# x and u of a fused attention and mixer kernel: turned by the crossbar DMA and added as PSUM is read

## The chip, the core and the metric

The kernel runs on one core of one Trainium2 chip. The metric is device time in microseconds (us), the median of several executions; the profile is one further execution taken by the hardware profiler.

## The reference

Causal attention over 8 batches of 8 heads, 576 positions of 64 elements, with a decay from the running sum of `max(s, 0)`; its output x (8 x 576 x 512) goes through a low-rank mix over the sequence and a two-layer ReLU network, each with a residual:

```python
cum = np.cumsum(np.maximum(s, 0.0), axis=-1)
scores = scale * q @ k^T + np.minimum(-(cum[i] - cum[j]), 0.0)     # causal
attn = softmax(scores);  x = attn @ v                              # heads side by side: 512 wide
h = x.transpose(0, 2, 1) @ U @ V                                   # rank 32, over the 576 positions
u = x + h.transpose(0, 2, 1)
out = u + np.maximum(u @ w_ch1, 0.0) @ w_ch2                       # 512 -> 2048 -> 512
```

## The kernel before

**Attention, two heads at a time.** A pair n is two heads of one batch; there are 32 pairs, four per batch. For each head `diagonal` (token D, matmul at L254) and `below` (E, L254) make the transposed scores in PSUM. ScalarE exponentiates them into the tiles `pT` (d, f, m and, once a pair, l: L319). VectorE masks the diagonal blocks (k, K: L322). `values` (A, L333) multiplies with v in 15 small matmuls, and `divide` (a, L348 and L349) writes the normalised x in bf16 into `x_sb`, positions on the partitions.

**The mix, one pair (128 channels) at a time.** `mix_in` (U, L363) multiplies x by U in five matmuls; `mix_keep` (u, L374) copies the result `ux` out of PSUM. The transposed u of the pair is then built in PSUM as x^T plus the low-rank part. `mix_x` (X, L381) turns x with four matmuls against the identity, each 128 wide. `mix_out` (Y) turns the last 64 positions (L392) and adds `ux` times V on top (L401, 512 and 64 columns). `mix_done` (y, L408 and L409) copies the sum into `uT`, which holds u^T of all 8 batches.

**The network, 512 tokens at a time.** Nine groups g. `widen` (L418) makes 16 tiles of the hidden layer, four matmuls of 512 columns each, followed by a ReLU on ScalarE (L425) into `hT`. `narrow` makes four output tiles of 128 tokens: 16 matmuls of 512 columns each (L435), then four matmuls of u^T against the identity (L447), which put u itself, positions on the partitions again, on top of the sum. `finish` copies the sum out (L458) and SyncE stores it.

**What sets the order.** Instructions are recorded in an order written out by hand, and each engine runs its own in that order. `SEQ` is the order for batches 0 and 1, `PAIR` the step repeated for n = 8 to 33: in step n the scores and exponentials of pair n, the values of pair n-2 (A-2, A-1 for its two heads) and the mix of pair n-2. A token `F` lets the network go on by one piece (four matmuls of L418 or of L435); `e` does so from pair 16 on; `r` records the ReLU or the copy-out that such a piece left pending. `p` spins idle matmuls (L498) early on, to keep TensorE working. `G` records a VectorE transpose (L238) of later q and k and, after every second one, four SyncE DMAs (`slot<-turned`, L244). Four PSUM buffers `pscore` serve the scores, four buffers `pwork` all the rest.

**The queues.** GpSimd issues the loads of q, k, v and weights in the order of `LOADS`. SyncE issues, in program order, the slot DMAs (L244), the rows of the decay (L162) and the stores of the output (L459).

Of the kernel before, what the change touches and what calls it, by code (L numbers as in the profile page):

```python
# [16 lines left out]
ALU = mybir.AluOpType  # L17
# [3 lines left out]
def kernel(  # L21
# [63 lines left out]
    uT = consts.tile([128, 4, B * S], BF16)  # L85
    staged = [[], []]
    for c, src0 in enumerate((q_0, k_0)):
        staged[0].append([src0[:, 0:4, :], src0[:, 4:8, :]])
        staged[1].append(
            [  # L90
                uT[:TP, 2 * c + i, 2 * S : 2 * S + 4 * TT * D].rearrange("p (h t) -> p h t", h=4)
                for i in range(2)
            ]
        )
    spare = [uT[:, dt, 2 * S + 4 * TT * D : 2 * S + 4 * TT * D + 2 * S] for dt in range(3)]
# [246 lines left out]
    def divide(h):  # L342
        b = h // H
        if b not in x_of:
            x_of[b] = work.tile([128, 5, DM], BF16, tag="x_sb", name="x_sb")
# [3 lines left out]
        nc.vector.tensor_tensor(  # L349
            x_of[b][:, :, ds(h % H * D, D)],  # L350
            po[:, :, 0:D],
            rec.to_broadcast([128, 5, D]),
            op=ALU.mult,
        )

    def x_part(n, t):
        return x_of[n // PB][:, t, ts(n % PB, 128)]

    def mix_in(n):
        up = pwork()  # L360
# [16 lines left out]
    def mix_x(n):  # L377
        ut = pwork()
        mix_of[n].append(ut)
        for t in range(4):  # L380
# [6 lines left out]
                skip_group_check=True,  # L387
            )

    def mix_out(n):  # L390
        up, ux, ut = mix_of[n]
        nc.tensor.matmul(  # L392
            up[:, 128:192],
            lhsT=x_part(n, 4),
            rhs=identity[:, :64],
            start=True,
            stop=False,
            skip_group_check=True,
        )
        for dst, lo, hi in ((ut, 0, 512), (up[:, 128:192], 512, S)):  # L400
            nc.tensor.matmul(  # L401
                dst, lhsT=ux, rhs=V_sb[:, lo:hi], start=False, stop=True, skip_group_check=True
            )

    def mix_done(copy, n):
        up, ux, ut = mix_of.pop(n)
        b, hp = divmod(n, PB)
        copy(uT[:, hp, ds(b * S, 512)], ut)  # L408
        copy(uT[:, hp, ds(b * S + 512, 64)], up[:, 128:192])  # L409

    hidden = {}

    def widen(g):
        hT = hidden[g] = work.tile([128, NF, 512], BF16, tag="hT", name="hT")
        for nf in range(NF):
            f1 = pwork()
            for kt in range(4):
                nc.tensor.matmul(  # L418
                    f1,
                    lhsT=w1_sb[nf // 4][:, kt, ds(nf % 4 * 128, 128)],  # L420
                    rhs=uT[:, kt, ds(g * 512, 512)],
                    start=(kt == 0),
                    stop=(kt == 3),
                )
            pending.append(lambda nf=nf, f1=f1: nc.scalar.activation(hT[:, nf, :], f1, RELU))  # L425
            del f1
            yield

    def narrow(g):
        hT = hidden.pop(g)  # L430
        for i in range(4):
            f2 = pwork()
            tok = g * 512 + i * 128
            for nf in range(NF):
                nc.tensor.matmul(  # L435
                    f2,
                    lhsT=hT[:, nf, ds(i * 128, 128)],
                    rhs=w2_sb[nf // 4][:, nf % 4, :],
                    start=(nf == 0),
                    stop=False,  # L440
                    skip_group_check=True,
                )
                if nf % 4 == 3 and nf < NF - 1:
                    pending.append(None)
                    yield
            for dt in range(4):
                nc.tensor.matmul(  # L447
                    f2[:, ds(dt * 128, 128)],
                    lhsT=uT[:, dt, ds(tok, 128)],
                    rhs=identity,  # L450
                    start=False,
                    stop=(dt == 3),
                    skip_group_check=True,
                )

            def finish(f2=f2, tok=tok):
                o_sb = work.tile([128, DM], FP32, tag="o_sb", name="o_sb", bufs=3)
                nc.vector.tensor_copy(o_sb, f2)  # L458
# [56 lines left out]
    def queue(n):  # L515
# [18 lines left out]
        "a": divide,  # L534
        "U": mix_in,
        "X": mix_x,
        "Y": mix_out,
        "t": take,
        "u": mix_keep,
# [9 lines left out]
    def play(tokens, pair=None):  # L549
        for token in tokens.split():  # L550
# [8 lines left out]
            if pair is not None and kind in "DEdfmkAaTtlKUXYuyG":  # L559
# [101 lines left out]
    def begin_v(i):  # L661
# [18 lines left out]
    SEQ = (  # L680
# [12 lines left out]
    )  # L693
    PAIR = (
        "D0 d0 U-2 uV-2 X-2 F r E0 k0 f0 G1 m0 F r D1 d1 Y-2 yV-2 F r E1 k1 f1 G1 m1 l0 F r A-2 "
        "K0 a-2 e r A-1 a-1 F r F r e r "
    )

    with tc.manual_schedule():
# [14 lines left out]
        queue(100 + NG - 1)  # L714
        while feed():
            follow()
        follow()


# [28 lines left out]
```

## Time and profile before

| what | value |
|---|---|
| median of 3 runs | 389.23 us (389.22 to 389.81) |
| the profiled execution's own time | 392.76 us |
| its span, first to last instruction | 391.0 us |
| mean granted TensorE clock | 0.978 |
| DMA packets | 76158, 36.79 MB |

A profile's page gives busy time by engine, the span in 40 slices, the DMA queues, the chain of work that ended last, and groups of instructions by line. Each row of a group reads: line, engine, operation, tiles, shapes and count, then busy time and the mean duration of one, then the idle time ahead of it and who ended that. The duration of a matmul is its whole passage through the array; matmuls overlap, so what one costs TensorE is the distance from start to start in the timeline. A windows view gives busy time of each engine in a stretch, the granted clock, and the DMA's share.

### The profile page before, as it was taken

To read this page: it belongs to the slowest core of one execution; us is meant where nothing else is said; L and a number is where in the kernel's file an instruction comes from. 1 tells how busy PE (TensorE), PEld (TensorE's weight loads), DVE (VectorE), ACT (ScalarE), POOL (GpSimd) and SP (SyncE) were. 2 spreads that over 40 slices of the span, in tenths; PEclk is the share of its full clock that TensorE was granted. 3 is DMA by queue.
4 is the path that set the end of the run, shared out by engine and by line. 5 is a ranking of instruction groups with operands and counts; after the bars stand their busy time and mean duration, and the time that the engine had idled before them with its cause. 6 is when DMAs were issued, how large, how long until landed. Compare 5 with 4: busy or idle time off the path is not lost.

```text
span 391.0 us, 8307 instructions
## 1 busy us (share of the span) xinstructions
PE 377.9 (97%) x3303; PEld 219.3 (56%) x3359; DVE 202.5 (52%) x429; ACT 207.7 (53%) x402; POOL 108.8 (28%) x175
## 2 busy tenths in 40 slices
PE   6998999999999999999999999999999999999995
PEld 2457557655666556555566555655655554444442
DVE  8348555795767676665566556655633332011011
ACT  7267899259634786347633773377337701611610
POOL 8795428147273072308040710000000000000000
PEclk9569999999999999999999999999999999999999
DMA  7999999469799589829682892211210002002002
GB/s 92 176 202 160 177 161 114 87 129 195 111 173 135 109 103 84 150 86 124 64 150 86 105 81 88 75 46 34 60 55 27 2 28 80 2 27 80 2 27 80
DMA packets 76158, 36.79 MB, mean 94 GB/s; under 512 B 60672, under 2 KB 67872, under 8 KB 76120
## 3 DMA queue, kind: packets, MB, share of 16 engines
q0 software_dynamic: 65616, 18.43, 52.5%
q1 hardware_dynamic: 10504, 17.83, 15.4%
q8 instruction: 26, 0.43, 0.5%
q14 instruction: 12, 0.10, 0.1%
HBM read 37.51 MB, written 10.03 MB: 122 GB/s over the span
## 4 chain that ended last, share of the span: by engine, by line
PE 90%; DVE 4%; DMA 2%; issue 2%; POOL 1%; SPq 0%; ACT 0%; ACTq 0%; POOLq 0%
PE pwork L418 31%; PE pwork L435 30%; PE pscore L254 11%; PE pwork L333 7%; PE pwork L363 2%; PE pwork L447 2%; PE pwork L401 2%; PE pwork L381 2%; DMA hT<-in_k_dram 1%; PE pscore L263 1%; DVE slot L224 1%; PE pwork L212 1%; DVE x_sb L349 1%; POOL hT L109 1%; DMA slot<-turned 1%
## 5 line engine op out<-in xcount | busy, mean ns | idle before, releaser
L319 ACT ACTIVATE pT<-pscore 128x512 bf16<-128x512 f32 (+1 forms) x224 | 113.3, 557 | 78.2 <-PE pscore L254 68.9
L418 PE MATMUL pwork<-uT,w_sb 128*128 128x512 bf16 x552 | 136.8, 379 | 2.0 <-DVE uT L408 0.7
L435 PE MATMUL pwork<-w_sb,hT 128*128 128x512 bf16 x547 | 135.2, 379 | 1.5
L425 ACT ACTIVATE hT<-pwork 128x512 bf16<-128x512 f32 x144 | 86.5, 605 | 70.2 <-PE pwork L418 68.7
L418 PEld LDWEIGHTS <-w_sb 128*128 128x128 bf16 x576 | 52.3, 98 | 50.3
L435 PEld LDWEIGHTS <-hT 128*128 128x128 bf16 x576 | 52.2, 98 | 50.3
L254 PE MATMUL pscore<-slot 128*128 128x128 bf16 (+5 forms) x576 | 70.1, 245 | 0.1
L458 DVE COPY o_sb<-pwork 128x512 f32<-128x512 f32 x36 | 24.9, 691 | 83.4 <-PE pwork L447 83.2
L254 PEld LDWEIGHTS <-slot 128*128 128x128 bf16 (+1 forms) x576 | 43.9, 99 | 32.3 <-issue 3.9
L238 DVE STREAM_TRANSPOSE turned<-qk_sd 128x576 bf16<-128x576 bf16 x48 | 54.6, 1141 | 0.7
L127 POOL DMA_DIRECT2D qk_sd<-in_q_dram x48 | 27.0, 570 | 96.8 <-DVE turned L238 90.6
L333 PEld LDWEIGHTS <-pT 128*128 128x128 bf16 x960 | 35.8, 98 | 9.3 <-issue 0.4
L333 PE MATMUL pwork<-v_slot,pT 128*128 128x65 bf16 x960 | 38.4, 193 | 0.3 <-DVE slot L224 0.3
L322 DVE TENSOR_TENSOR pT<-pT,keep 128x512 bf16<-128x512 bf16 (+1 forms) x84 | 29.3, 353 | 16.4 <-ACT pT L319 16.1
L349 DVE TENSOR_TENSOR x_sb<-pwork,rec 128x320 bf16<-128x320 f32 x64 | 31.5, 492 | 2.2
L408 DVE CAST uT<-pwork 128x512 bf16<-128x512 f32 x27 | 18.6, 690 | 24.7 <-PE pwork L401 24.7
L127 POOL DMA_DIRECT2D qk_sd<-in_k_dram x48 | 27.2, 573 | 8.9 <-DMA w_sb<-in_moe_w_ch_dram 5.1
L135 POOL DMA_DIRECT2D v_slot<-in_v_dram x32 | 28.4, 898 | 2.3 <-DMA v_slot<-in_v_dram 1.5
L224 DVE COPY slot<-pwork 64x576 bf16<-64x576 bf16 x21 | 16.5, 796 | 17.6 <-PE pwork L212 14.7
L374 DVE CAST ux<-pwork 128x128 bf16<-128x128 f32 x26 | 7.5, 287 | 26.5 <-PE pwork L363 26.5
L348 DVE RECIPROCAL rec<-pwork 128x5 f32<-128x5 f32 x64 | 12.2, 190 | 11.2 <-PE pwork L333 10.9
L447 PEld LDWEIGHTS <-uT 128*128 128x128 bf16 x144 | 11.1, 98 | 8.5
(80 smaller groups left out, 192.3 us busy)
## 6 DMA issues: line engine op xcount, KB each, us to landing
out_dram<-o_sb SPq DMA_DIRECT2D x36, 256.0 KB
slot<-turned SPq DMA_DIRECT2D x96, 72.0 KB
v_slot<-in_v_dram POOLq DMA_DIRECT2D x32, 128.0 KB, 6.9
w_sb<-in_moe_w_ch_dram POOLq DMA_DIRECT2D x8, 512.0 KB, 11.7
qk_sd<-in_q_dram POOLq DMA_DIRECT2D x48, 72.0 KB, 3.8
qk_sd<-in_k_dram POOLq DMA_DIRECT2D x48, 72.0 KB, 4.0
uT<-in_q_dram POOLq DMA_DIRECT2D x2, 288.0 KB, 8.1
uT<-in_k_dram POOLq DMA_DIRECT2D x2, 288.0 KB, 9.0
```

The source lines that it names most:

```text
L127: nc.gpsimd.dma_start(out=qk_t[g][ds(32 * a, 32), c, :].rearrange("p (n f) -> p n f", n=6), in_=src[g // 2, 4 * (g % 2) + a].rearrange("(n ...
L135: nc.gpsimd.dma_start(out=vt[:, t, :, 0:D], in_=v[b, :, ds(t * 128, 128), :].rearrange("h p d -> p h d"),)
L238: nc.vector.transpose(turned[:, e, c].rearrange("p (n m t) -> p n t m", n=6, t=3), src[:, c].rearrange("p (n t e d) -> p e n t d", n=6, t= ...
L254: nc.tensor.matmul(dst, lhsT=head_of(h)[0:rows, ds(S + j * 128, 128)], rhs=head_of(h)[0:rows, lo:hi], start=start, stop=stop and not bias, ...
L319: nc.scalar.activation(dst, src, EXP, scale=scale)
L322: nc.vector.tensor_tensor(p, p, m, op=ALU.min)
L333: nc.tensor.matmul(po[:, i, :], lhsT=p_of(h)[:, ds(spot(j, i), 128)], rhs=v_slots[h // H % 3][:, j, h % H, :], start=(j == 0), stop=(j == ...
L349: nc.vector.tensor_tensor(x_of[b][:, :, ds(h % H * D, D)], po[:, :, 0:D], rec.to_broadcast([128, 5, D]), op=ALU.mult,)
L418: nc.tensor.matmul(f1, lhsT=w1_sb[nf // 4][:, kt, ds(nf % 4 * 128, 128)], rhs=uT[:, kt, ds(g * 512, 512)], start=(kt == 0), stop=(kt == 3),)
L425: pending.append(lambda nf=nf, f1=f1: nc.scalar.activation(hT[:, nf, :], f1, RELU))
L435: nc.tensor.matmul(f2, lhsT=hT[:, nf, ds(i * 128, 128)], rhs=w2_sb[nf // 4][:, nf % 4, :], start=(nf == 0), stop=False, skip_group_check=True,
L458: nc.vector.tensor_copy(o_sb, f2)
```

## The change

**x.** From batch 2 on (n >= 8) the five matmuls that turn x (L381, L392) are gone. A new token `x` (`turn_x`) has SyncE issue one crossbar transpose per pair, a DMA from `x_sb` (128 x 640, bf16) to one of three buffers `xT`. `mix_out` now starts its PSUM sum from `ux` times V alone, and `mix_done` adds `xT` on VectorE as it reads PSUM. `x_sb` is laid out by pair, so that a pair's x is contiguous.

**u.** From group 1 on (UB = 1) the four matmuls per output tile that put u on the sum (L447) are gone. At the start of `widen(g)` SyncE issues one crossbar transpose per group, from `uT` (128 x 2048) to one of two buffers `u_sb`; `finish` adds `u_sb` on VectorE as it reads PSUM.

**Buffers.** `uT` now holds a ring of four groups instead of all batches; the 576 columns of a pair are cut where a group ends, so the two matmuls with V have 384 and 192 columns in batch 2, 320 and 256 in batch 3, and so on, instead of 512 and 64. The second batch's staging of q and k lies in the new tile `stage`, whose space the transposes use later; scratch rows of the decay have tiles of their own.

**Orders.** `SEQ` and `LOADS` are other orders of nearly the same tokens: idle spins are 25 matmuls instead of 17 (first eight and five and four; now twelve ahead of the first q and k transposes, eight behind them, then three and two), and weights w3, w2 and w1 come ahead of the second half of batch 1's q and k. In `PAIR` both D0 and E0 come first, the network goes on in threes rather than by one, `x-1` follows the division of the pair one step younger than the one that is mixed, and Y and y stand late in the step; `ux` is copied by ScalarE (uA) instead of VectorE (uV).

```diff
+    uT = consts.tile([128, 4, 4, 512], BF16)
+    stage = consts.tile([128, 16 * TT * D], BF16, name="stage")
+    u_sb = [stage[:, ts(i, 2048)].rearrange("p (d i c) -> p d i c", d=4, i=4) for i in range(2)]
...
+    def turn_x(n):
+        nc.sync.dma_start_transpose(
+            out=xT[n % 3], in_=x_of[n // PB][:, n % PB].rearrange("p t c -> p (t c)")
+        )
...
+        mixed = n >= 2 * PB
+        cut = 512 - 64 * (n // PB)
+        if mixed:
+            mix_of[n].append(pwork())
...
+        for dst, lo, hi in pieces:
+            nc.tensor.matmul(
+                dst, lhsT=ux, rhs=V_sb[:, lo:hi], start=mixed, stop=True, skip_group_check=True
+            )
...
+                if b >= 2:
+                    turned = xT[n % 3].rearrange("p t c -> p (t c)")
+                    nc.vector.tensor_add(dst, got[:, p - lo : e - lo], turned[:, p:e])
+                else:
+                    copy(dst, got[:, p - lo : e - lo])
...
+    def turn_u(g):
+        nc.sync.dma_start_transpose(
+            out=u_sb[g % 2].rearrange("p d i c -> p (d i) c"),
+            in_=uT[:, g % 4].rearrange("p d c -> p (d c)"),
+        )
...
     def widen(g):
+        if g >= UB:
+            turn_u(g)
...
-            for dt in range(4):
+            for dt in range(4 if g < UB else 0):
                 nc.tensor.matmul(
                     f2[:, ds(dt * 128, 128)],
...
+                    nc.vector.tensor_tensor(
+                        o_sb.rearrange("p (d c) -> p d c", d=4),
+                        f2.rearrange("p (d c) -> p d c", d=4),
+                        u_sb[g % 2][:, :, i, :],
+                        op=ALU.add,
+                    )
...
-        "v0 u0 s0 w0 u1 w1 k0 x0 s1 v2 w2 w3 v1 x3 x1 x2 q4 q5 "
+        "u1 v0 u0 k0 w0 s0 w3 w2 w1 s1 x2 v1 x0 x1 x3 q4 v2 q5 "
...
-        "p1 p3 p4 T0 p5 Z0 T1 tA0 tV1 T3 p4 T2 tA0 D0 tA2 tV1 E0 T5 d0 f0 tV3 tV2 m0 D1 tV3 d1 "
+        "p7 p5 Z0 T0 tA0 tA0 p8 T3 T1 tA1 T2 tV3 D0 d0 tV3 tV2 tA1 p3 E0 D1 p2 d1 T5 f0 E1 tV2 "
...
-        "D0 d0 U-2 uV-2 X-2 F r E0 k0 f0 G1 m0 F r D1 d1 Y-2 yV-2 F r E1 k1 f1 G1 m1 l0 F r A-2 "
-        "K0 a-2 e r A-1 a-1 F r F r e r "
+        "D0 E0 r d0 A-2 U-2 G1 r e k0 F a-2 G1 D1 r A-1 f0 uA-2 e r l0 d1 F m0 a-1 x-1 r F r E1 "
+        "f1 k1 Y-2 r e K0 r yA-2 m1 F F "
```

On VectorE, one step of the later batches, before (`ux` and the two copies into `uT` are L374, L408 and L409; the copy-out of an output tile is L458):

```order
L374 CAST ux<-pwork 128x128
L322 TENSOR_TENSOR pT_77<-pT_77,keep 128x512
L238 STREAM_TRANSPOSE turned<-qk_sd 128x6x3x32
L408 CAST uT<-pwork 128x512
L409 CAST uT<-pwork 128x64
L322 TENSOR_TENSOR pT_77<-pT_77,keep 128x512
L238 STREAM_TRANSPOSE turned<-qk_sd 128x6x3x32
L458 COPY o_sb<-pwork 128x512
L322 TENSOR_TENSOR pT_77<-pT_77,keep 128x2x64
L348 RECIPROCAL rec<-pwork 128x5
L349 TENSOR_TENSOR x_sb<-pwork,rec 128x5x64
```

And now, a step of the same kind (the adds into `uT` are L439, the output tile's add is L502, the divide L355 and L356):

```order
L329 TENSOR_TENSOR pT_77<-pT_77,keep 128x512
L355 RECIPROCAL rec<-pwork 128x5
L356 TENSOR_TENSOR x_sb<-pwork,rec 128x5x64
L245 STREAM_TRANSPOSE turned<-qk_sd 128x6x3x32
L502 TENSOR_TENSOR o_sb<-pwork,stage 128x512
L355 RECIPROCAL rec<-pwork 128x5
L356 TENSOR_TENSOR x_sb<-pwork,rec 128x5x64
L329 TENSOR_TENSOR pT_77<-pT_77,keep 128x512
...
L329 TENSOR_TENSOR pT_77<-pT_77,keep 128x2x64
L439 TENSOR_TENSOR uT<-pwork,stage 128x192
L439 TENSOR_TENSOR uT<-pwork,stage 128x384
L245 STREAM_TRANSPOSE turned<-qk_sd 128x6x3x32
```

The writes into `uT` have moved behind both divides of the step, the cast of `ux` has left VectorE, and each add reads `stage`, which a DMA has written.

On SyncE, one batch of the later ones, before:

```order
L162 DMA slot_80<-rows_hbm 4x4x1152
L244 DMA slot_80<-turned 32x1152 x8
L459 DMA out_dram<-o_sb 128x512 x2
L162 DMA slot_81<-rows_hbm 4x4x1152
L244 DMA slot_81<-turned 32x1152 x4
```

And now (the transposes of x are L398, that of u is L444):

```order
L508 DMA out_dram<-o_sb 128x512
L398 DMA_TRANSPOSE stage<-x_sb 128x5x128
L508 DMA out_dram<-o_sb 128x512
L251 DMA slot_81<-turned 32x1152 x4
...
L444 DMA_TRANSPOSE stage<-uT 128x16x128
L169 DMA slot_79<-rows_hbm 4x4x1152
L251 DMA slot_79<-turned 32x1152 x4
L398 DMA_TRANSPOSE stage<-x_sb 128x5x128
```

The same stores and slot DMAs stand there with a transpose of x between them at every pair, and one of u at every group, ahead of the next slot DMAs.

More of the change, by code (lines that the diff above doesn't have):

```diff
@@ L84 @@
     w2_sb = [consts.tile([128, 4, DM], BF16, name=f"w2_sb{i}") for i in range(4)]
-    uT = consts.tile([128, 4, B * S], BF16)
+    uT = consts.tile([128, 4, 4, 512], BF16)
+    stage = consts.tile([128, 16 * TT * D], BF16, name="stage")
+    u_sb = [stage[:, ts(i, 2048)].rearrange("p (d i c) -> p d i c", d=4, i=4) for i in range(2)]
+    xT = [
+        stage[:, ds(4096 + 640 * i, 640)].rearrange("p (t c) -> p t c", t=5) for i in range(3)
+    ]
+    spare = [consts.tile([128, 2 * S], BF16, name=f"spare{i}") for i in range(3)]
     staged = [[], []]
@@ L344, in divide @@
         if b not in x_of:
-            x_of[b] = work.tile([128, 5, DM], BF16, tag="x_sb", name="x_sb")
+            x_of[b] = work.tile([128, 4, 5, 128], BF16, tag="x_sb", name="x_sb")
         po = po_of.pop(h)
@@ L400, in mix_out @@
[L400 to L409, printed above, removed]
+        if not mixed:
+            nc.tensor.matmul(
+                up[:, 128:192],
+                lhsT=x_part(n, 4),
+                rhs=identity[:, :64],
+                start=True,
+                stop=False,
+                skip_group_check=True,
+            )
+            pieces = ((ut, 0, 512), (up[:, 128:192], 512, S))
+        elif cut >= S - cut:
+            pieces = ((ut[:, 0:cut], 0, cut), (up[:, 128 : 128 + S - cut], cut, S))
+        else:
+            pieces = ((up[:, 128 : 128 + cut], 0, cut), (ut[:, 0 : S - cut], cut, S))
@@ new lines, in mix_out, with mix_done @@
+        for dst, lo, hi in pieces:
+            nc.tensor.matmul(
+                dst, lhsT=ux, rhs=V_sb[:, lo:hi], start=mixed, stop=True, skip_group_check=True
+            )
+        mix_of[n] = pieces
+    def mix_done(copy, n):
+        b, hp = divmod(n, PB)
+        cut = 512 - 64 * b
+        for got, lo, hi in mix_of.pop(n):
+            for p, e in ((lo, min(hi, cut)), (max(lo, cut), hi)):
+                if p >= e:
+                    continue
+                at = b * S + p
+                dst = uT[:, at // 512 % 4, hp, ds(at % 512, e - p)]
+                if b >= 2:
+                    turned = xT[n % 3].rearrange("p t c -> p (t c)")
+                    nc.vector.tensor_add(dst, got[:, p - lo : e - lo], turned[:, p:e])
+                else:
+                    copy(dst, got[:, p - lo : e - lo])
@@ L439, in narrow @@
                     start=(nf == 0),
-                    stop=False,
+                    stop=g >= UB and nf == NF - 1,
                     skip_group_check=True,
@@ L558, in play @@
                 args, rest = (copy_of[rest[0]],), rest[1:]
-            if pair is not None and kind in "DEdfmkAaTtlKUXYuyG":
+            if pair is not None and kind in "DEdfmkAaTtlKUXYuyGx":
                 i = int(rest)
```

31 lines of the change are left out of this document (15 added, 16 removed), and 22 rows, old and new, of the table SEQ.

## The prediction

> **What bounds the kernel now.** I read the page's head and its chain first, then the windows by stage, then the timeline around the matmuls that go.
>
> ```profile
> span 391.0 us, 8307 instructions
> PE 377.9 (97%) x3303; PEld 219.3 (56%) x3359; DVE 202.5 (52%) x429; ACT 207.7 (53%) x402; POOL 108.8 (28%) x175
> PE 90%; DVE 4%; DMA 2%; issue 2%; POOL 1%; SPq 0%; ACT 0%; ACTq 0%; POOLq 0%
> ```
>
> The columns of a window are its length, busy time and count by engine, granted clock, DMA share and GB/s.
>
> ```profile
> 0.00:10.00 10.00, 6.35 (x32) 2.96 (x33) 8.31 (x24) 7.44 (x7) 8.73 (x19) 0.97 0.73 93
> 10.00:26.00 16.00, 16.00 (x79) 7.58 (x77) 4.59 (x7) 6.08 (x11) 13.09 (x21) 0.50 1.69 186
> 26.00:42.00 16.00, 14.00 (x240) 11.22 (x241) 12.76 (x29) 12.22 (x28) 10.43 (x14) 0.98 1.96 176
> 42.00:120.00 78.00, 77.32 (x733) 46.79 (x745) 52.19 (x101) 52.68 (x109) 37.02 (x60) 1.00 1.19 142
> 130.00:330.00 200.00, 198.21 (x1846) 118.08 (x1879) 110.12 (x245) 105.35 (x208) 35.04 (x55) 1.00 0.47 75
> 330.00:391.00 61.00, 56.82 (x284) 26.76 (x287) 6.22 (x9) 19.10 (x32) 0.00 (x0) 1.00 0.10 39
> ```
>
> TensorE (PE) carries 90% of the chain and is busy 198.2 of 200 us from 130 to 330, with VectorE (110) and ScalarE (105) half free. There, TensorE work that goes is time that goes, as long as no wait takes its place. The start is another stage: from 10 to 26 us TensorE is never idle, but at a granted clock of 0.50; from 26 to 42 VectorE and ScalarE are at 80% and 76% and share the bound.
>
> **What the removed matmuls cost.** Their listed durations (219 and 193 ns) overlap with their neighbours'; from start to start the timeline gives:
>
> ```profile
> 312.76 0.44 PE L363 MATMUL pwork<-x_sb,U_sb 128*128 128x128 bf16 x5
> 313.04 0.39 PE L381 MATMUL pwork<-identity,x_sb 128*128 128x128 bf16 x4
> 313.26 1.89 PE L435 MATMUL pwork<-w_sb,hT 128*128 128x512 bf16 x8
> 314.99 0.19 PE L392 MATMUL pwork<-identity,x_sb 128*128 128x64 bf16 x1
> 315.01 0.41 PE L401 MATMUL pwork<-V_sb,ux 128*128 128x512 bf16 x2
> 315.26 1.89 PE L435 MATMUL pwork<-w_sb,hT 128*128 128x512 bf16 x8
> 316.99 0.39 PE L447 MATMUL pwork<-identity,uT 128*128 128x128 bf16 x4
> 317.21 0.62 PE L333 MATMUL pwork<-v_slot,pT 128*128 128x65 bf16 x15
> 317.66 1.02 PE L435 MATMUL pwork<-w_sb,hT 128*128 128x512 bf16 x3
> ```
>
> - Four L447 take 316.99 to 317.21, 0.22 us. 8 of 9 groups lose four such blocks: 32 x 0.22 = 7.0 us.
> - Four L381 take 313.04 to 313.26, 0.22 us: 24 pairs x 0.22 = 5.3 us.
> - One L392 takes 0.02 to 0.03 us: 24 x 0.025 = 0.6 us.
> - The two L401 keep 576 columns however they are cut, 315.01 to 315.26: nothing.
>
> Sum: 12.9 us off TensorE, nearly all of it in the stage where it sets the time. Of the 32 blocks, eight lie in the last two groups, behind the attention, where nothing else competes.
>
> **What comes in its place on VectorE and ScalarE.**
>
> ```profile
> L458 DVE COPY o_sb<-pwork 128x512 f32<-128x512 f32 x36 | 24.9, 691 | 83.4 <-PE pwork L447 83.2
> L349 DVE TENSOR_TENSOR x_sb<-pwork,rec 128x320 bf16<-128x320 f32 x64 | 31.5, 492 | 2.2
> L408 DVE CAST uT<-pwork 128x512 bf16<-128x512 f32 x27 | 18.6, 690 | 24.7 <-PE pwork L401 24.7
> L374 DVE CAST ux<-pwork 128x128 bf16<-128x128 f32 x26 | 7.5, 287 | 26.5 <-PE pwork L363 26.5
> L319 ACT ACTIVATE pT<-pscore 128x512 bf16<-128x512 f32 (+1 forms) x224 | 113.3, 557 | 78.2 <-PE pscore L254 68.9
> L425 ACT ACTIVATE hT<-pwork 128x512 bf16<-128x512 f32 x144 | 86.5, 605 | 70.2 <-PE pwork L418 68.7
> ```
>
> The copies become two-input adds that read PSUM. No such add of 512 columns is in the trace; the nearest row, L349, has two inputs and takes 492 ns for 320 columns, and a copy takes 691 for 512. A line through 0.15 us with 1.07 ns a column fits both, so I give the add 0.69 us: no change; the bound above is 492 x 512/320 = 0.79 us, 0.1 us more on an engine that is half free. I find no reason for it to be quicker than the copy. `ux` goes to ScalarE: 24 x 0.27 = 6.5 us there, as much off VectorE.
>
> ScalarE is the one to watch. A step in which the network widens holds seven exponentials (113.3 / 32 = 3.5 us), eight ReLUs (8 x 0.60 = 4.8) and now `ux` (0.3): 8.6 us. The step itself, 10.0 us before (the 200 us window holds 20), falls to about 9.6. That is 90% of it. I walked one such step by hand with these durations, TensorE pieces of 0.86 us (four matmuls of 512 columns), 0.45 (one `values`), 0.7 (D0 and E0) and 0.2 us for a handover. The ReLUs finish 0.1 to 0.8 us ahead of the piece that needs their `pwork` buffer, except one (the first piece after Y), which is 0.1 us late. E0 of the next step has 0.5 us in hand on the last exponential, m1. `values` of the next step now waits for the late add y, but that ends 2 us ahead. So about 0.1 us a widening step, 12 of them: +1.2 us, between 0 and 0.4 us a step (5 us); I take +1.5, nearest the walk.
>
> **The transposes.** 24 of x (160 KB each) and eight of u (512 KB) join SyncE's queue, where each waits for its data with everything behind it. What they take the trace does not show. The nearest rows are the queues, q0 with short pieces and q1, which is SyncE's, and one slot DMA that the chain ran through:
>
> ```profile
> q0 software_dynamic: 65616, 18.43, 52.5%
> q1 hardware_dynamic: 10504, 17.83, 15.4%
> 124.68 2.57 DMA slot<-turned
> ```
>
> A q0 packet (281 bytes) takes 52.5% x 16 x 391 / 65616 = 50 ns of one of 16 engines. If a transpose moves in pieces of 256 bytes (a row of a 128-column block), x is 640 of them, 640 x 50 / 16 = 2.0 us, and u 2048, 6.4 us; with some 2.5 us to land (the slot DMA) 4.5 and 9 us. If it moves in 32-byte pieces (16 positions of one column), it is eight times that, 16 and 51 us. I take the near end, because the slot DMA, SBUF to SBUF on the same queue like these, shows no such penalty. What hides it: x is asked for after a-1, half-way through a step, and added at the end of the next step, 12 us later by the walk; u is asked for when a group starts and added after 16 pieces and a first output tile, at least 20 x 0.86 = 17 us later. What is queued behind: the slot DMAs, which feed scores a full step (10 us) later, and the stores, for which no one waits but the three output buffers. So at the near end nothing is late: 0.
>
> The Trainium skill, "VectorE: DVE Perf Modes", section on the three transpose paths, speaks against the change: 390 ns for a 128x128 bf16 block on TensorE, 1309 ns by the crossbar DMA. If that were a rate, it would be an estimated 6.5 us for x and 21 us for u; in the trace TensorE does such a block in 0.055 us, since its matmuls overlap, so its figure for TensorE is not what this kernel pays; for the DMA's no run here shows one. By it the sum would be that of the last rival but one, an estimated 408 us.
>
> **The start.** Spins are reordered: twelve instead of eight ahead of the first transposes, eight instead of five behind them, then three and two inside the first scores, for four.
>
> ```profile
> 6.00:7.00 1.00, 1.00 (x10) 0.58 (x8) 0.97 (x2) 0.98 (x3) 1.00 (x3) 1.00 1.15 138
> 7.00:8.00 1.00, 0.40 (x6) 0.16 (x3) 0.95 (x4) 0.99 (x2) 0.93 (x3) 1.00 1.14 141
> 8.00:9.00 1.00, 0.00 (x0) 0.00 (x0) 1.00 (x6) 0.49 (x1) 1.00 (x2) 1.00 0.92 115
> 9.00:10.00 1.00, 0.24 (x4) 0.25 (x5) 0.99 (x2) 0.00 (x0) 1.00 (x2) 0.73 1.18 149
> 1.29 3.60 PE L498 MATMUL pwork<-warm 128*128 128x512 bf16 x8 [1.29 <-DVE warm L105]
> 9.98 1.91 PE L498 MATMUL pwork<-warm 128*128 128x512 bf16 x4
> ```
>
> Before, the clock is full at 6 to 9 us, TensorE then stands for most of 7.0 to 9.8 us waiting for the next k, and the clock falls to half and stays there until 26. Now twelve spins (0.43 us each at first) last to about 6.3, eight more to about 8.4, and the gap is 1.4 us instead of 2.4. I think it likelier than not that the clock survives it. Then the 16 us at 0.50 shrink towards what ScalarE needs: 6.1 + 12.2 = 18.3 us of work from 10 to 42, at the 76% of the last window 24 us, ending near 34.5 instead of 42: at most -7.5, less some 1.1 us for the five late spins. If the clock falls all the same, the five spins cost 2.1 us where four cost 1.9: about +0.4. Between these ends I take -4: the first group of the network also waits for copies on VectorE, at 80%.
>
> The Trainium skill, "TensorE: Matmul & The Clock Gate", Part 1, has the gate open after about 3.4 us of sustained work. By that alone the clock would have been back near 14 us, for TensorE is not idle from 10 on, the start would hold 6 us less to gain, and the sum would be an estimated 377 us; the row shows 0.50 until 26, and the row decides.
>
> **The sum**, against the profiled execution's own 392.76 us (span 391.0): -12.9 (matmuls) - 4.0 (start) + 1.5 (handovers) + 0 (transposes) = -15.4, 377.4 us. The median of the runs shown is 389.23, 3.5 us below the profiled run, so 373.8 us.
>
> **Rivals.**
> - *The clock falls at the start as before.* For: the gap for k is still there. Against: it is shorter, after more work. 389.2 - 12.9 + 0.4 + 1.5 = 378.2.
> - *ScalarE takes over in widening steps.* For: 90% of the step, and work now comes in bursts of three pieces, after which two of four `pwork` buffers are held by the mix and `values`. Against: the walk. If each of 12 steps loses 0.7 us instead of 0.1, 8.4 us instead of 1.5, without a gain at the start: 389.2 - 12.9 + 0.4 + 8.4 = 385.
> - *The transposes land late (slower).* For: their price is unknown by a factor of eight, and DMA is the one resource that the change loads. The point: a batch asks for 4 x + u = 14.4 us of all 16 engines at 256 bytes in a batch of 38.5 us, and 115 us at 32. Around 100 bytes (37 us, u alone some 16) u pushes the first x of the next batch past its add; VectorE then stands, `values` behind it for want of a buffer, and TensorE with them. At 5 us late in each of six batches: 378.2 + 30 = 408; with 64 bytes (57.6 us a batch, 19 too many) 378.2 + 115 = 493. The 21 us by the skill's page would fall in this case.
> - *It does nothing*: waits fill what was removed, 389. Against: TensorE waits for 1.8 us in 200 now.
>
> **Chances.** Forecast 0.48; clock falls 0.25; ScalarE 0.10; transposes late 0.13; nothing 0.04. The range 369.0 to 382.5 takes in the forecast with its start term from -7.5 to 0 and steps from 0 to 5 us (369 to 381), the fallen clock, and part of the ScalarE case; it leaves out late transposes, nothing, and the rest: 0.2. Faster (by over 0.2%, about what a measurement of this kernel can tell from no change): 0.48 + 0.25 + 0.10 + 0.01 = 0.84; same 0.03; slower 0.13.
>
> **What would show it.** Right: TensorE still near 99% busy from 130 us on; windows of 10 us where the clock is 1.00 from about 6 us; L439 and L502 at 0.69 us with next to no wait for a DMA. Wrong: TensorE waiting for L439, or L439 waiting for a transpose of more than 12 us; ScalarE without idle time in widening steps and TensorE waiting for L466; a clock of 0.50 at 10 to 26 us.

## The result, and the profile after

| | before | after |
|---|---|---|
| median | 389.23 us (388.57 to 389.81) | 378.91 us (375.77 to 382.26, four executions) |
| ratio, 95% interval | | 0.9661 [0.9633, 0.9689] |
| profiled execution, its own time | 392.76 us | 376.26 us |
| TensorE clock, mean | 0.978 | 0.995 |

The ratio leaves out the two longer executions after (381.57 and 382.26 us, at a clock of 0.982 and 0.977), so it is not the quotient of the medians. A second measurement of the changed kernel (below) gave 376.62 us; over its ten executions the median is 377.0. Forecast: 373.8, range 369.0 to 382.5. The sign, the range and the largest term held. Two other terms did not: the transposes, put at nothing, cost about 3 us, and the gain at the start depends on something that the change leaves to each execution.

A slip first: `A-2` and `A-1` in step n are the two heads of pair n-1, not n-2 as the section on the kernel has it. The mix (U-2, Y-2, y-2) is that of pair n-2, and `x-1` turns pair n-1.

The page's head, its chain by engine, and the two queues that matter:

```profile
span 374.5 us, 7844 instructions
PE 361.8 (97%) x3069; PEld 206.0 (55%) x3119; DVE 192.4 (51%) x406; ACT 210.7 (56%) x429; POOL 108.3 (29%) x175
q0 software_dynamic: 65616, 18.43, 61.2%
q1 hardware_dynamic: 43272, 25.96, 36.2%
PE 82%; DMA 8%; DVE 5%; issue 2%; ACT 1%; POOL 1%; SPq 1%; DVEq 0%; ACTq 0%; POOLq 0%
```

DMA has risen from 2% to 8% of the chain. SyncE's queue q1 carries 43272 - 10504 = 32768 packets more, and 8.13 MB: 24 x 640 + 8 x 2048 = 31744 pieces of 256 bytes (8.13 MB), and 32 more for each of the 32 transposes. That is the near end of the prediction. q0 carries the same packets and bytes as before, but they occupy 61.2% of the engines instead of 52.5%: the same loads take longer. Without the transposes (below) the share is 54.9%, so this is not the other order of the loads.

The windows by stage (length, busy time and count by engine, granted clock, DMA share, GB/s):

```profile
0.00:10.00 10.00, 8.51 (x50) 4.11 (x50) 8.30 (x24) 8.24 (x8) 8.43 (x19) 1.00 0.69 92
10.00:26.00 16.00, 15.15 (x175) 9.53 (x175) 10.03 (x16) 11.89 (x24) 14.93 (x23) 1.00 1.56 173
26.00:42.00 16.00, 15.12 (x184) 10.11 (x186) 9.75 (x22) 11.81 (x26) 6.04 (x9) 1.00 1.54 194
42.00:120.00 78.00, 74.94 (x746) 46.41 (x756) 54.13 (x112) 50.75 (x111) 43.88 (x72) 0.98 1.50 165
120.00:130.00 10.00, 9.21 (x96) 5.46 (x94) 7.25 (x17) 5.64 (x14) 0.86 (x2) 1.00 1.17 195
130.00:315.00 185.00, 183.52 (x1581) 105.38 (x1608) 96.70 (x212) 103.25 (x219) 34.19 (x54) 1.00 0.92 108
```

From 130 us on TensorE is as full as before (183.5 of 185 us). From 10 to 26 us the clock is 1.00, not 0.50. But from 42 to 120, where TensorE was busy 77.3 of 78 us, it now stands 3 us; the 0.8 from 120 to 130 stood there before too (9.20 of 10 us busy).

To place the difference I measured both traces from matmul to matmul: when the first of a pair's scores, or of a group's tiles, starts. "Lost" is the time of a stretch beyond its matmuls at 0.417 ns a column plus 2.5 ns each. That is an estimate, a line that fits the distances from start to start in the traces: 0.86 us for four matmuls of 512 columns, 0.22 for four of 128, 0.45 for 15 of 65.

| stretch (start of its last mark) | before | after | lost before | lost after |
|---|---|---|---|---|
| to the first tile of the network | 41.79 us | 35.12 us | 20.1 | 11.0 |
| pair 8 to pair 12 | 116.98 | 110.08 | 0.07 | 4.1 |
| pair 12 to pair 16 | 149.60 | 139.56 | 1.0 | 1.1 |
| then four pairs each, to pair 28 | 40.79 long | 38.89 long | 0.1 each | 0.1 each |
| whole span | 391.0 | 374.5 | | |

So -9.1 at the start, +4.1 between pairs 8 and 12, and the other -11.5 is matmuls that are gone, net of eight more spins (8 x 0.21 = 1.7): 13.2. In the steady stretches four pairs fell by 1.90 us; the prediction's prices give 16 L381 as four blocks (0.88), four L392 (0.1) and 4.5 output tiles (0.99): 1.97.

Where the 4.1 us are, from the waits on DMAs and the chain in order of time:

```profile
DVE uT L439 <- DMA stage<-x_sb: 7.5, 3, 3.4
PE pscore L261 <- DMA slot<-turned: 2.4, 1, 2.4
PE pwork L459 <- DVE uT L439: 0.7, 1, 0.7
```

```profile
74.44 3.19 DMA qk_sd<-in_q_dram
...
86.07 8.15 DMA slot<-turned
...
110.60 5.84 DMA out_dram<-o_sb
116.45 7.89 DMA stage<-x_sb
```

A slot DMA on the chain of before took 2.57 us; the one on this chain takes 8.15, and the scores that it feeds wait 2.4 us for it. What stands on SyncE ahead of it, and what TensorE does then:

```profile
76.51 4.87 SPq L444 DMA_TRANSPOSE stage<-uT  x1
81.48 0.67 SPq L508 DMA_DIRECT2D out_dram<-o_sb  x1
82.24 3.10 SPq L251 DMA_DIRECT2D slot<-turned  x4
85.44 0.53 SPq L537 DMA_DIRECT2D rows_hbm<-spare  x1
86.07 3.61 SPq L251 DMA_DIRECT2D slot<-turned  x4
```

```profile
90.04 1.89 PE L459 MATMUL pwork<-uT,w_sb 128*128 128x512 bf16 x8
94.35 1.49 PE L261 MATMUL pscore<-slot 128*128 128x128 bf16 x9 [2.43 <-DMA slot<-turned]
95.64 1.03 PE L340 MATMUL pwork<-v_slot,pT 128*128 128x65 bf16 x15
```

The first transpose of u (group 1) holds SyncE for 4.87 us. The gap that follows is 2.4 us; after it 15 matmuls of `values` take 1.03 us, where they took 0.62 in the prediction's timeline: the clock is at half from 94.0 to 97.4, another 1.6 us. The two are the 4.1. The three waits of L439 for x fall later, at 117, 124 and 187 us, and in those stretches as much is lost as before. No add of u (L502) waited for its transpose.

### The profile page after: what moved, and what is told of

It reads as the page before. It is cut to its first block, busy times and chain, and to the rows that moved or that the text cites. A ratio compares the mean times of both kernels' runs of the same rounds, so it can differ in the third digit from the quotient of the medians.

```text
span 374.5 us, 7844 instructions
## 1 busy us (share of the span) xinstructions
PE 361.8 (97%) x3069; PEld 206.0 (55%) x3119; DVE 192.4 (51%) x406; ACT 210.7 (56%) x429; POOL 108.3 (29%) x175
## 3 DMA queue, kind: packets, MB, share of 16 engines
q0 software_dynamic: 65616, 18.43, 61.2%
q1 hardware_dynamic: 43272, 25.96, 36.2%
## 4 chain that ended last, share of the span: by engine, by line
PE 82%; DMA 8%; DVE 5%; issue 2%; ACT 1%; POOL 1%; SPq 1%; DVEq 0%; ACTq 0%; POOLq 0%
PE pwork L459 30%; PE pwork L476 28%; PE pscore L261 10%; PE pwork L340 6%; DMA slot<-turned 2%; PE pwork L370 2%; DMA stage<-x_sb 2%; DVE turned L245 2%; PE pwork L423 2%; DMA out_dram<-o_sb 2%; ACT pT L326 1%; DMA hT<-in_k_dram 1%; PE pscore L270 1%; DMA qk_sd<-in_q_dram 1%; POOL hT L116 1%
## 5 line engine op out<-in xcount | busy, mean ns | idle before, releaser
L459 PE MATMUL pwork<-uT,w_sb 128*128 128x512 bf16 x553 | 131.8, 379 | 1.9 <-DVE uT L439 0.7
L476 PE MATMUL pwork<-w_sb,hT 128*128 128x512 bf16 x552 | 129.1, 379 | 1.2
L476 PEld LDWEIGHTS <-hT 128*128 128x128 bf16 x576 | 54.5, 98 | 58.1
L459 PEld LDWEIGHTS <-w_sb 128*128 128x128 bf16 x576 | 54.4, 98 | 57.4 <-issue 0.3
L261 PE MATMUL pscore<-slot 128*128 128x128 bf16 (+5 forms) x576 | 65.0, 242 | 3.3 <-DMA slot<-turned 2.4
L502 DVE TENSOR_TENSOR o_sb<-pwork,stage 128x512 f32<-128x512 f32 x32 | 21.9, 685 | 73.8 <-PE pwork L476 70.9
L261 PEld LDWEIGHTS <-slot 128*128 128x128 bf16 (+1 forms) x576 | 41.0, 98 | 32.8 <-issue 6.7
L356 DVE TENSOR_TENSOR x_sb<-pwork,rec 128x320 bf16<-128x320 f32 x64 | 31.5, 491 | 2.3
L439 DVE TENSOR_TENSOR uT<-pwork,stage 128x384 bf16<-128x384 f32 (+7 forms) x48 | 19.8, 452 | 23.1 <-PE pwork L423 15.6
L355 DVE RECIPROCAL rec<-pwork 128x5 f32<-128x5 f32 x64 | 12.1, 189 | 23.8 <-PE pwork L340 23.6
L231 DVE COPY slot<-pwork 64x576 bf16<-64x576 bf16 x20 | 15.7, 796 | 11.5 <-PE pwork L219 6.9
L370 PE MATMUL pwork<-x_sb,U_sb 128*128 128x128 bf16 x160 | 14.5, 222 | 0.3 <-DVE x_sb L356 0.2
L423 PE MATMUL pwork<-V_sb,ux 128*128 128x64 bf16 (+7 forms) x62 | 12.6, 283 | 0.1
## 6 DMA issues: line engine op xcount, KB each, us to landing
stage<-in_q_dram POOLq DMA_DIRECT2D x2, 288.0 KB, 10.2
```

What stands on the lines that cost most here:

```text
L261: nc.tensor.matmul(dst, lhsT=head_of(h)[0:rows, ds(S + j * 128, 128)], rhs=head_of(h)[0:rows, lo:hi], start=start, stop=stop and not bias, ...
L356: nc.vector.tensor_tensor(x_of[b][:, h % H // 2, :, ts(h % 2, D)], po[:, :, 0:D], rec.to_broadcast([128, 5, D]), op=ALU.mult,)
L370: nc.tensor.matmul(up[:, 0:128], lhsT=U_sb[:, t, :], rhs=x_part(n, t), start=(t == 0), stop=(t == 4), skip_group_check=True,)
L459: nc.tensor.matmul(f1, lhsT=w1_sb[nf // 4][:, kt, ds(nf % 4 * 128, 128)], rhs=uT[:, g % 4, kt, :], start=(kt == 0), stop=(kt == 3),)
L476: nc.tensor.matmul(f2, lhsT=hT[:, nf, ds(i * 128, 128)], rhs=w2_sb[nf // 4][:, nf % 4, :], start=(nf == 0), stop=g >= UB and nf == NF - 1, ...
```

## The experiments

Three theories. **Overlap**: a transpose costs nothing once the loads are through, and costs where they still run, u of group 1 above all. **Late**: any transpose that comes close to its add costs, all through the kernel. **Spins**: the start is won by the reordered spins (rival: it varies from execution to execution, whatever the spins).

**Without any transposes.** `turn_x` and `turn_u` issue nothing and the adds read tiles of weights instead, so the outputs lack x and u from there on.

```diff
     def turn_x(n):
-        nc.sync.dma_start_transpose(
+        return
...
-                    turned = xT[n % 3].rearrange("p t c -> p (t c)")
+                    turned = w1_sb[n % 3].rearrange("p t c -> p (t c)")
...
     def turn_u(g):
-        nc.sync.dma_start_transpose(
+        return
...
-                        u_sb[g % 2][:, :, i, :],
+                        w2_sb[g % 2][:, :, ts(i, 128)],
```

> The changed kernel with no crossbar transposes: the adds read weights that lie in SBUF already instead of the turned x and u, so the output lacks both residuals from batch 2 and group 1 on. It gives what the transposes cost in all. Theory (they cost about 4 us, all of it by making loads late once, between pairs 8 and 12): about 372. If they cost nothing: 376. If they also slow the later steps: under 371.

Measured: 371.54 us (371.3 to 371.87), ratio 0.9540 [0.9483, 0.9597]; nothing lost between pairs 8 and 16 beyond 0.25 us. Its chain by engine:

```profile
PE 96%; DVE 2%; ACT 1%; issue 0%; ACTq 0%
```

DMA is gone from it. Against the changed kernel's executions with a clock of 0.998 or more (374.05, 374.05, 375.5, 375.77: mean 374.8) the transposes cost about 3 us; against its median, 5.5. All four executions here kept a clock of 0.997 or more, as six of the changed kernel's ten kept 0.995: four of four by luck has a chance of 0.6^4 = 0.13, so whether the transposes have a hand in the spread of the clock is not settled.

**Without u's, and without x's.** Each leaves out one of the two kinds by the lines above, so that one output lacks u from group 1 on, the other x from batch 2 on.

> The changed kernel without the crossbar transposes of u: finish adds weights that lie in SBUF instead, so the output lacks u from group 1 on; the transposes of x stay. Theory (the 512 KB transposes of u are what makes loads and slot DMAs late): 372 to 373 at a clock near 1.00, close to the kernel without any. Rival (x's do): 376.

> The changed kernel without the crossbar transposes of x: mix_done adds weights that lie in SBUF, so the output lacks x in u from batch 2 on; the transposes of u stay. Theory (u's are to blame): 375 to 376 at a clock near 1.00. Rival (x's are): 372 to 373.

Measured: without u 373.11 us (372.46 to 376.22), ratio 0.9596 [0.9558, 0.9635]; lost between pairs 8 and 12 only 0.1, between 12 and 16 0.9. Without x 377.97 (375.78 to 381.12), ratio 0.9711 [0.9663, 0.976]; lost 1.9 and 0.15. So the loss of pairs 8 to 12 is u's. The one of pairs 12 to 16 goes with x's, but not always: with x in place and u from group 2 on (below) one profile lost 0.15 there and the other 1.15. The total of the second run is no price of x, because of its start: its clock was 0.57 from 10 to 26 us (below).

**The changed kernel again**, unchanged, beside these.

> The changed kernel itself, more often, to see its executions beside their granted clock. Theory (two amounts add: the clock lost at the start, and clock and time lost where late transposes leave TensorE idle between pairs 8 and 16): times from 375 at a clock near 1.00 to 382 at 0.98, more spread than the kernel without transposes (371.3 to 371.9). Rival (the spread is all of the start): the same spread as the kernel before, about 5 us between clock 0.976 and 1.000.

Measured: 376.62 us (374.05 to 380.25), ratio 0.9665 [0.9622, 0.9707]; lost between pairs 8 and 12 1.9, against 4.1 in the first profile. The loss is real, its size varies: here the scores waited 1.7 us for the slot DMA and the clock stayed at 1.00, so that the half clock of the first profile is missing.

**u from group 2 on**, twice. Group 1 keeps its 16 matmuls (0.9 us); the transpose at 76 us is gone.

```diff
-    UB = 1
+    UB = 2
```

> The changed kernel, but the first group whose u is turned by DMA is group 2 instead of group 1: one 512 KB transpose less, at about 76 us, and 16 more matmuls of L488 (4 x 0.22 = +0.9 us). Theory (the transpose of u at 76 us delays the loads of q, k and v behind it and through them the scores of pair 8, which cost the changed kernel some 4 us between pairs 8 and 12): the wait of 2.4 us for a slot DMA at 92 us and the half clock after it go, 376 - 4 + 0.9 = about 373. Rival (the new order of the loads alone makes them late): the wait stays, about 377.

> The changed kernel with u turned by DMA from group 2 on instead of group 1, taken a second time with more rounds. If the transpose of group 1's u, at 76 to 84 us, is what delays the loads that are still running, this kernel loses 0.1 to 0.5 us instead of 2 to 4 between pairs 8 and 12, pays 0.9 us of matmuls for it, and its median is 1.5 to 3 us below the changed kernel's 376.6 to 378.9: 374 to 376. If the difference seen before was chance, the median is that of the changed kernel plus or minus 0.5 us.

Measured: 376.71 us (373.13 to 378.39), ratio 0.9661 [0.9588, 0.9734], and 376.9 (373.64 to 378.32), ratio 0.9674 [0.9629, 0.9719]. Between pairs 8 and 12 both lose 0.10 us: the gap is gone, as Overlap says. The medians did not fall by the expected 1.5 to 3 us, because in 8 of these 10 executions the clock was 0.991 or less. The two with 0.999 or more took 373.13 and 373.64, below each of the changed kernel's ten. The gain shows there, though in two executions only; in the others the start hides it.

**u of group 1 later.** The transpose is issued after 13 of the 16 hidden tiles.

```diff
-        if g >= UB:
+        if g > UB:
             turn_u(g)
...
             del f1
+            if g == UB and nf == 12:
+                turn_u(g)
             yield
```

> The changed kernel with the transpose of group 1's u issued after 13 of the 16 hidden tiles instead of ahead of the first, some 8 to 10 us later, when fewer loads remain. If it is the overlap with the loads that costs, the loss between pairs 8 and 12 falls from 1.9 to 4.1 us to 0.1 to 1.5, without the 0.9 us of matmuls of the two kernels above: median 373.5 to 375.5. If the loads are disturbed just as much there, or if the output's add now waits for the transpose (the first add comes four pieces, some 4 to 6 us, later), the loss stays at 2 us or more and L502 shows a wait for its DMA; median 376 to 379.

Measured: 374.61 us (373.78 to 378.21), ratio 0.9637 [0.9594, 0.9679]: the median as Overlap has it. Its profile fell on its slowest execution (378.21) and shows 0.1 us lost between pairs 8 and 12, but 4.0 between 12 and 16, the chain passing through

```profile
103.29 8.90 DMA stage<-x_sb
...
120.07 6.24 DMA stage<-x_sb
```

So x can be late there too, and cost more there than in any other profile of the new pair order, x twice (next) aside.

**x twice.** On top of UB = 2 each transpose of x from pair 16 on, in the steady stage, is issued twice into the same buffer; the second waits for the first.

```diff
+        if n >= 16:
+            nc.sync.dma_start_transpose(
+                out=xT[n % 3], in_=x_of[n // PB][:, n % PB].rearrange("p t c -> p (t c)")
+            )
```

> The kernel with u from group 2 on, with every transpose of x from pair 16 on (batch 4, after the loads) issued twice, 16 further transposes of 160 KB into the same place. If the transposes cost only where loads run beside them, four pairs still take 38.9 us in the steady stage, TensorE loses 0.1 us in it, and the time is the same within 0.5 us. If the room of 12 us is nearly used up (transfer or SyncE's queue), the adds L439 wait for a DMA and each pair takes 0.3 us or more longer: 5 us or more in all.

Measured: 383.26 us (380.05 to 385.2), ratio 0.9819 [0.9759, 0.9879]. Overlap's "same within 0.5 us" missed. But it is one pair in four that pays: pairs 16 to 20 lost 5.1 us, 20 to 24 4.2, and 24 to 28 0.1. TensorE's own waits behind the adds are 6.0 of these; most of the rest is a clock of 0.50 from 178.8 to 185.7 us, behind the first of them. The chain at the first, and the waits of the adds (L443 here):

```profile
165.10 7.36 DMA stage<-x_sb
172.48 6.83 DMA stage<-x_sb
```

```profile
DVE uT L443 <- DMA stage<-x_sb: 18.1, 5, 5.4
```

Two in a row took 14.2 us, more than the room. In the changed kernel's steady steps that is 10.5 to 10.8 us (x issued at 233.4 us and added at 244.2, for one), not the 12 that I had walked. The first of the two stood 7.36 us ahead of the second where q, k and v of later batches were being loaded (q0's packets end at about 220 us), and 2.66 us at 227 us. Overlap is right about when a transpose is slow, but loads run further than I had thought, and in the changed kernel's profile x took up to 9.0 us (the add at 187 us waited 3.4 for it).

**The old pair order with the transposes.** `PAIR` as before, with `x-1` right behind `a-1`, the earliest place that it has there; the new spins and loads stay.

```diff
-        "D0 E0 r d0 A-2 U-2 G1 r e k0 F a-2 G1 D1 r A-1 f0 uA-2 e r l0 d1 F m0 a-1 x-1 r F r E1 "
-        "f1 k1 Y-2 r e K0 r yA-2 m1 F F "
+        "D0 d0 U-2 uV-2 F r E0 k0 f0 G1 m0 F r D1 d1 Y-2 yV-2 F r E1 k1 f1 G1 m1 l0 F r A-2 "
+        "K0 a-2 e r A-1 a-1 x-1 F r e r e r "
```

> The changed kernel with the pair step in the order of before, less the token X, and with x-1 put behind a-1: x leaves near the end of a step and is added in the middle of the next, some 6 us later instead of 12. Theory (a transpose of x takes 4 to 8 us from issue to landing while loads run): the add L439 waits for a DMA in most steps of batches 2 to 5, TensorE behind it, 380 to 390. Rival (the order is indifferent): 376.

Measured: 400.06 us (398.96 to 405.68), ratio 1.0263 [1.0226, 1.03]: slower than before the change, and than the 380 to 390 expected. Its waits of the adds, and of the values behind them (the profile is of the slowest execution, and its clock is at 0.50 for 13.7 us between 124 and 255 us as well):

```profile
DVE uT L439 <- DMA stage<-x_sb: 44.1, 13, 6.4
PE pwork L340 <- DVE uT L439: 15.3, 6, 4.3
```

Here the rival "transposes land late" stands in full: the add waits for x, `values` for the add. With the same matmuls removed, the order of the step decides between 0.966 and 1.026. The old order without transposes was not run, so what else of the 23 us it may bring is open.

**The spins alone.** The kernel before with the new spins, and the changed kernel with the old ones.

```diff
-        "p1 p3 p4 T0 p5 Z0 T1 tA0 tV1 T3 p4 T2 tA0 D0 tA2 tV1 E0 T5 d0 f0 tV3 tV2 m0 D1 tV3 d1 "
+        "p7 p5 T0 p8 Z0 T1 tA0 tV1 T3 T2 tA0 D0 tA2 tV1 p3 E0 T5 d0 f0 tV3 tV2 m0 D1 p2 tV3 d1 "
```

```diff
-        "p7 p5 Z0 T0 tA0 tA0 p8 T3 T1 tA1 T2 tV3 D0 d0 tV3 tV2 tA1 p3 E0 D1 p2 d1 T5 f0 E1 tV2 "
+        "p8 Z0 T0 tA0 tA0 p5 T3 T1 tA1 p4 T2 tV3 D0 d0 tV3 tV2 tA1 E0 D1 d1 T5 f0 E1 tV2 "
```

> The kernel before with nothing changed but the idle spins of the start: 25 as in the changed kernel (twelve, eight, three, two) instead of 17. Theory (the spins keep the clock, and the clock is what the start gained): clock near 1.00 from 10 to 26 us where it was 0.50, first matmul of L418 some 4 to 6 us earlier than 41.75, 384 to 385. Rival (the start gained by its other order of loads and copies): 389 to 391.

> The changed kernel with 17 spins as before: eight ahead of the first transposes, five behind them, four ahead of the first scores, none inside. Theory: the clock falls to 0.50 near 10 us and stays there until past 20; 376 + 6 = about 382. Rival (the start's gain has nothing to do with the spins): 374 to 376, a little faster for 8 spins less.

Measured: 389.44 us (386.41 to 391.4), ratio 0.9995 [0.9958, 1.0032]; and 377.72 (375.79 to 378.83), ratio 0.9694 [0.9634, 0.9753]. In the median the spins give nothing either way, so both runs miss Spins. Three of the ten executions of the first kept a clock of 1.0 and took 386.4 to 387.4 us; the others had 0.982 to 0.991. In the second run's profile the clock fell (0.79 from 10 to 26 us) and the first group came 2.5 us later than in the changed kernel's, but only 0.5 us was lost between pairs 8 and 12. A later start could meet fewer loads there, but the run without x, whose first group came 6.2 us later, lost 1.9; so this is not shown.

**Five more spins.** UB = 2, and five idle matmuls more ahead of k's transposes.

```diff
-        "p7 p5 Z0 T0 tA0 tA0 p8 T3 T1 tA1 T2 tV3 D0 d0 tV3 tV2 tA1 p3 E0 D1 p2 d1 T5 f0 E1 tV2 "
+        "p7 p5 Z0 T0 tA0 tA0 p8 p5 T3 T1 tA1 T2 tV3 D0 d0 tV3 tV2 tA1 p3 E0 D1 p2 d1 T5 f0 E1 tV2 "
```

> The kernel above with five more idle matmuls (1.1 us at full clock) behind the first key transposes, so that TensorE is not idle when k is late. If the short gap for k decides whether the clock stays full from 10 to 26 us, every execution keeps a granted clock near 1.0 there, the executions lie within 1.5 us of each other, and the fastest is at most 1 us slower than that of the kernel above; median 373 to 375. If the clock at the start is set by something else, the five matmuls cost up to 1 us, executions with 0.5 to 0.8 at 10 to 26 us still occur, and the median is that of the kernel above plus 0.5 to 1.

Measured: 375.21 us (373.33 to 375.8), ratio 0.9631 [0.9599, 0.9663]. Five of six executions had a clock of 0.998 or more and the sixth 0.991, so neither every clock nor the spread (2.5 us) is as expected. Without the five spins two of ten kept 0.995 with UB = 2, but five of six did with u of group 1 later, whose first 70 us are the same instructions. Over all runs with that start it was 22 of 38 (not counting x twice and the old pair order, whose clock falls later as well). At such a rate five or six of six come by luck with a chance of about one in five. How the gap for k reads, first in the kernel before, then in the changed one, without x, UB = 2 (its second run), and UB = 2 with five spins more (timeline of TensorE; the idle time ahead is in brackets):

```profile
9.76 0.42 PE L212 MATMUL pwork<-identity,hT 96*128 96x96 bf16 x3 [1.77 <-DMA hT<-in_k_dram]
```

```profile
8.32 0.81 PE L219 MATMUL pwork<-identity,hT 96*128 96x96 bf16 x15 [0.20 <-DMA hT<-in_k_dram]
```

```profile
9.37 0.81 PE L219 MATMUL pwork<-identity,hT 96*128 96x96 bf16 x15 [1.45 <-DMA hT<-in_k_dram]
```

```profile
8.44 0.81 PE L219 MATMUL pwork<-identity,hT 96*128 96x96 bf16 x15 [0.45 <-DMA hT<-in_k_dram]
```

```profile
9.19 0.81 PE L547 MATMUL pwork<-warm 128*128 128x512 bf16 x3
9.83 0.55 PE L219 MATMUL pwork<-identity,hT 96*128 96x96 bf16 x9
```

And the window from 10 to 26 us of the last three, in the same order:

```profile
10.00:26.00 16.00, 16.00 (x86) 7.47 (x83) 5.81 (x8) 6.61 (x12) 14.50 (x22) 0.57 1.52 170
```

```profile
10.00:26.00 16.00, 15.64 (x131) 9.22 (x132) 7.50 (x13) 9.45 (x18) 14.96 (x23) 0.79 1.57 174
```

```profile
10.00:26.00 16.00, 15.15 (x161) 9.31 (x160) 9.44 (x15) 11.04 (x22) 14.50 (x23) 1.00 1.53 174
```

The fourteen profiles line up: no gap for k, or up to 0.28 us, clock 1.00 (six profiles); 0.45 to 0.77 us, 0.79 (six); 1.45 us and more, 0.57 and 0.50 (two). The gap has two ends that vary. With the changed kernel's loads and a gap, k lands and its transposes start between 8.3 and 9.4 us. And the spins ahead of them end at another time in each execution, because they go from 0.43 to 0.22 us each (half clock to full) earlier or later: the first twelve took 4.7 us in the changed kernel's profile and 5.3 in the one without transposes (L542), where the other eight then lasted until k was there.

```profile
1.29 4.71 PE L547 MATMUL pwork<-warm 128*128 128x512 bf16 x12 [1.29 <-DVE warm L112]
```

```profile
1.29 5.30 PE L542 MATMUL pwork<-warm 128*128 128x512 bf16 x12 [1.29 <-DVE warm L112]
```

The profile with five spins more is one of the late kind (5.30 us), so it doesn't show the five closing a gap. That the gap decides the start fits all fourteen profiles, but the time of that step to full clock moves with it, and the two were not separated. More spins seem to raise the odds: with the old ones 2 of 34 listed executions of the kernel before kept 0.995 (one of 1381 us left out) and none of four of the changed one, with the new ones 3 of 10 and 6 of 10. Five more are not shown to raise them further. The median with them is 1.8 us below the changed kernel's 377.0, but the intervals of the two ratios overlap, and it has u from group 2 on besides. Both it and the one with u of group 1 later are far below the kernel before.

## Why the prediction was right, and where it was not

**Matmuls, -12.9: right.** 13.2 by the table of stretches, and 1.90 a batch where the prices give 1.97. TensorE stayed full behind them, so what was removed came off the time.

**Adds at the price of copies: right.** Two-input adds that read PSUM, the output's and u^T's:

```profile
L502 DVE TENSOR_TENSOR o_sb<-pwork,stage 128x512 f32<-128x512 f32 x32 | 21.9, 685 | 73.8 <-PE pwork L476 70.9 <-PE pwork L423 2.8
L439 DVE TENSOR_TENSOR uT<-pwork,stage 128x384 bf16<-128x384 f32 (+7 forms) x48 | 19.8, 452 | 23.1 <-PE pwork L423 15.6 <-DMA stage<-x_sb 7.5
```

685 ns for 512 columns, where the line through L349 and the copy gave 0.69 us and the other end was 0.79.

**Handovers, +1.5: nothing.** In the steady stretches 0.1 us was lost in four pairs, before and after; a step took 10.2 us and then 9.7. The rival "ScalarE takes over" did not happen.

**The transposes, 0: this step failed.** Their form was right (256-byte pieces), and the price of a piece even too high: with the queues quiet x moves in 0.92 us and is through 2.1 us after its issue (20 ns a piece and engine, not 50), u in 2.6 and 3.9. By the Trainium skill, "VectorE: DVE Perf Modes", section on the three transpose paths, taken as a rate, x would need an estimated 6.5 us and u 21: these rows disagree when the queues are quiet. What failed was "So at the near end nothing is late". I compared each transpose alone with its own room and did not ask what it meets: up to about 220 us the loads of q0 use the same engines, x then takes 2.1 to 9.0 us, mostly over 3, and u 3.9 to 10.8, and the room of x was 10.5 us, not 12. What it costs is mostly not the add that waits but what stands behind it on SyncE and beside it on the engines: the slot DMA, and with it the scores. I had named that queue and dismissed it, since the slot feeds scores "a full step later". With u left out the loss between pairs 8 and 12 is 0.1 us, so u is its cause; whether it works by SyncE's 4.87 us or by the engines that it takes was not separated. Cost: about 3 us.

**The start, -4.0: the mechanism fits, its size a matter of the execution.** The prediction had the clock survive a gap of 1.4 us. In the profile the gap was 0.20, since k was there at 8.3 us and not at 9.8; the one profile of the new start with 1.45 fell to 0.57. That the clock held was in part luck. The profiled pair gained 9.1 us, 7.4 net of the eight spins' 1.7, about the bound of 7.5, since the profiled execution of before was one with the clock at half for all 16 us. The median of before (389.2) holds executions from 386.5 (clock 1.000) to 392.7 (0.978), so part of the gain was in it already; I had subtracted 3.5 us for that and the full 4 as well. Compared at a clock of 0.998 or more, before is 386.4 to 387.4 with either spins, after 374.8 by the mean above: -12. That is 13.2 of matmuls, less 3 of transposes, and a remainder of 2; 1.4 of it is seen at the start, where the first tile comes at 36.5 us in before with the new spins and at 35.1 after, presumably by the other order of loads and tokens.

**The sum.** 377.4 against 376.3 for the profiled execution came out close by luck, because errors cancelled: the start gave 3.4 us more net of its spins, the handovers cost 1.5 less, and the transposes took 4.1 in that execution. The median shows what did not cancel, 377.0 against 373.8.

**Late transposes, rival at 0.13.** Its mechanism is real, with the order of the step as the point that decides: 400 us with the old order, by adds that wait up to 6.4 us. My point of decision, the size of a piece, was the wrong one.

## What to carry to other kernels

Moving work from a full engine to the DMA pays what it takes off that engine, if the stretch between data ready and data used is sized by the time that a transfer takes beside the loads that run then, here up to four times the quiet one; count also what stands behind it on the issuing engine. When executions of one kernel differ by 2%, compare them at equal granted clock and look for a short wait early on.

## What the runs showed of the hardware

- A gap of 0.45 to 0.77 us at about 8 us was followed by a clock of 0.50 for some 7 us, and in all six profiles that came only at 15 us; whether the gap was its cause, and why it comes so late, was not tried. The Trainium skill, "TensorE: Matmul & The Clock Gate", Part 1, has the gate close after an idle window of about 3.4 us that runs freely; here 2.4 us sufficed at 92 us in one execution, and 1.7 us at the same place did not in another.
- A crossbar transpose holds SyncE for 1.2 us (x, up to 2.4) and 1.7 to 7.0 us (u) to be issued, the long ones while loads run.
- One kernel's executions differ with their mean granted clock: the changed kernel's ten lie between 374.05 us at 0.998 and 382.26 at 0.977.
